# Four neighbouring channels to a chunk row, alpha doubled on ScalarE, two queues for the last rows: one change to a two-branch kernel

## The chip, the core and the metric

The kernel runs on one core of a Trainium2 chip. Its time is the device time of one execution in microseconds (us). An execution under the profiler lists each instruction of the engines: TensorE (PE; its weight loads are PEld), VectorE (DVE), ScalarE (ACT), GpSimd (POOL) and the issuing queue SyncE (SP). A name with a q (SPq, ACTq, POOLq) stands for what the engine's queue does beside computing, issuing DMAs above all. The granted clock is the share of TensorE's full clock that it was given.

## What is computed

Two independent branches over 2048 positions and 640 channels are laid side by side in the output. Branch A is attention with 32 heads of 20 dimensions in a window of 8 keys, two positions apart:

```python
qkv = (x @ wqkv).reshape(B, S, 3, H, Dh)            # H = 32, Dh = 20
idx = pos[:, None] - (jnp.arange(8) * 2)[None, :]
attn = softmax(where(idx >= 0, einsum("bhsd,bhswd->bhsw", q, k[idx]) * scale, -1e9))
a = einsum("bhsw,bhswd->bhsd", attn, v[idx]).reshape(B, S, D) @ wo
```

Branch B is a state space convolution (S4) with 192 complex states a channel:

```python
dt = exp(log_dt)[:, None]
K = einsum("dn,dnl,dn->dl", C, exp(dt * A[:, :, None] * l), dt * B).real   # a filter of 2048 for each channel
y = irfft(rfft(u, 2L) * rfft(K, 2L))[:L] + u * Dskip
```

## The kernel before, in words

**Branch B** works in five chunks of 128 channels (NCH = 5, c = 0 to 4; LAST = 4). The 640 channels are split as g (4 groups of 160), u (4), t (8) and c (5, innermost): chunk c holds every fifth channel. On the partitions stand 32 rows (g, t) for each u. `load` (L122) brings each of the six parameter arrays with four DMAs, one for each u, on the queues of SP, ACT and GpSimd; a partition's five channels are neighbours in memory, one run of 5 x 192 elements. `decays` (L162) turns dt times A_re to columns on TensorE and writes alpha (float32, 4 x 48 numbers a partition and chunk). `fill` (L169) makes the phases on VectorE and moves them with DMAs, `weights` and `coefficients` make C times B.

For each chunk `exps_chunk` (L236) fills the table R on ScalarE with exponentials of multiples of alpha. From chunk 1 on it writes 2 alpha into the place of the previous chunk's alpha (L248, a GpSimd addition), and one ACTIVATE (L251) then reads both. `phase_table` (L267) makes sines in the tables TA and TX (TensorE L288 and L292, ScalarE L296). `small_half` (L310) multiplies tables on VectorE (PG, Q, X; all L317), `y_form` (L341) makes Y (L347), and `kgen_unit` (L351) contracts X and Y on TensorE (L360, L365) into 32 values of l1 by 64 of l0 for each of 8 t in 4 g: one of four units u of the filter K, copied by ScalarE into Ksb (L366). `fwd` (L369) is the forward transform, of u (`fwd_u`) or of K (`transform`): four pieces of eight channels in a first stage (TensorE L379, ScalarE L380), four in a second (L386, L387). Piece b reads channels 8b to 8b + 7 in the chunk's order, which for K is unit b. `products` and `inverse_a` (L408, L417) multiply the spectra and do half of the inverse transform into memory (Z). `times_d` (L436) multiplies half a chunk of u by Dskip into UD (one buffer, ten calls; VectorE L441), and GpSimd's queue stores it (L442).

**Branch A** then projects k, q and v on TensorE, makes products on VectorE and logits, softmax, and in `av_step` (L666) the products of attention and v (VectorE L679), summed on TensorE. `Inverse.part` (L757) is a piece of the second half of branch B's inverse transform: TensorE, a ScalarE copy into ysb (through L473), and after each third part four stores. `out_piece` (L707) is the projection by wo of a block of rows, with a copy into ob and a store of each of its row blocks (L728). From the twelfth piece on (`late`) all stores go by SP.

**The order of work.** A planner orders each engine's instructions by cost estimates, except what is wrapped in `keep_in_program_order` or `issue_after`. From `att.in_order()` on TensorE and ScalarE keep program order. There the loop over six groups of eight steps (L984 to L1009) puts in parts of the inverse transform and output pieces by hand: FILLS gives for a step n how many pieces of `rest` (output) and of `parts` (inverse) follow it; in group 0 the parts come ahead of the step's av_step. `sums` (the softmax's denominators for the second half) come at steps 8, 10, 12 and 14.

Of the kernel before, what the change touches and what calls it, by code (L numbers as in the profile page):

```python
# [10 lines left out]
A = mybir.AluOpType  # L11
ACT = mybir.ActivationFunctionType
# [4 lines left out]
NCH = 5  # L17
# [78 lines left out]
def partB_prep(tc, pools, prm):  # L96
# [12 lines left out]
    alpha = flat[:, 3616:5536].bitcast(f32).rearrange("p (c u w) -> p c u w", c=NCH, u=4)  # L109
    V.memset(early[96:128, :].bitcast(f32), 1.0019378662109375)  # L110
    V.memset(flat[96:128, 0:1536].bitcast(f32), 1.0019378662109375)
    ldt = pl.tile([128, NCH], bf16, name="ldt")
    lsrc = prm["B_log_dt"].rearrange("(g u t c) -> u g t c", g=4, u=4, t=8)
    late = tc.keep_in_program_order
    one = pl.tile([128, 2], f32, name="one")
    nc.gpsimd.memset(one[:], 0.0)
    for u in range(4):
        late((nc.scalar, nc.sync)[u % 2].dma_start(out=ldt[32 * u:32 * u + 32, :], in_=lsrc[u]))
    nat = {}
    F1n, F32n = table_consts_np()  # L120

    def load(nm):  # L122
        nat[nm] = (pl if nm == "B_A_re" else pd).tile([128, NCH, 192], bf16, name=nm, tag=nm)
        src = prm[nm].rearrange("(g u t c) n -> u g t (c n)", g=4, u=4, t=8)
        for u in range(4):
            queue = {"B_A_re": (nc.scalar, nc.sync)[u % 2], "B_A_im": nc.gpsimd, "B_B_im": nc.gpsimd, "B_C_im": nc.gpsimd, "B_C_re": (nc.gpsimd, nc.sync)[u // 2]}.get(nm, nc.sync)
            late(queue.dma_start(out=nat[nm][32 * u:32 * u + 32].rearrange("p c n -> p (c n)"), in_=src[u]))

    load("B_A_re")
    load("B_A_im")  # L130
# [8 lines left out]
    dtb = pl.tile([128, NCH], bf16, name="dtb")  # L139
    late(nc.scalar.activation(out=dtb[:], in_=ldt[:], func=ACT.Exp))  # L140
    dtc = pl.tile([128, NCH], f32, name="dtc")
    V.tensor_copy(out=dtc[:], in_=dtb[:])
    dts = pools["fft"].tile([128, NCH], f32, name="dts")
    V.tensor_scalar(out=dts[:], in0=dtc[:], scalar1=4.0 / 3.0, scalar2=None, op0=A.mult)
    id32 = cpool.tile([128, 32], bf16, name="id32", tag="id32")
# [90 lines left out]
def exps_chunk(tc, pools, B, c):  # L236
    nc = tc.nc
    flat = pools["tab"].tile([128, 9216], bf16, name="R", tag=f"R{c % 2}")
    RA = flat[:, 0:3072].rearrange("p (h g q a f) -> p h g q a f", h=2, g=2, a=8, f=4)
    RX = flat[:, 3072:9216].rearrange("p (q e f) -> p q e f", e=32, f=4)  # L240
    al = B["alpha"][:, c]
    by_half = al.rearrange("p (h v) (q f) -> p h (v q) f", h=2, f=4)
    src = al.rearrange("p u (q f) -> p (u q) f", f=4)
    nc.gpsimd.memset(flat[:, 0:3072].rearrange("p (x a f) -> p x a f", a=8, f=4)[:, :, 0, :], 1.0)
    nc.gpsimd.memset(RX[:, :, 31, :], 1.0)
    if c > 0:
        twice = B["alpha"][:, c - 1]
        nc.gpsimd.tensor_tensor(out=twice, in0=al, in1=al, op=A.add)  # L248
        both = B["alpha"][:, c - 1:c + 1]
        both = both.rearrange("p e u (q f) -> p (u q) e f", f=4)  # L250
    exp = lambda o, i, m: nc.scalar.activation(out=o, in_=i, func=ACT.Exp, scale=m)  # L251
# [12 lines left out]
    return RA, RX  # L264
# [171 lines left out]
def times_d(tc, pools, C, UDd, c, i):  # L436

    nc = tc.nc
    U = C["U"][:].rearrange("p l (ut c) -> p c l ut", c=NCH)[:, c]
    UD = pools["tabb"].tile([128, 32, 32], bf16, name="UD", tag="UD")  # L440
    tc.keep_in_program_order(nc.vector.tensor_tensor(out=UD[:], in0=U[:, 32 * i:32 * i + 32], in1=bc(C["Dsb"][:, c], 1, 32), op=A.mult))  # L441
    nc.gpsimd.dma_start(out=UDd[c, :, 1024 * i:1024 * i + 1024], in_=UD[:].rearrange("p l j -> p (l j)"))  # L442


def fwd_u(tc, pools, C, c, place):

    U = C["U"][:].rearrange("p l (ut c) -> p c l ut", c=NCH)[:, c]
    return fwd(tc, pools, C, (lambda ut: U[:, :, ut]), 0, pools["fft"], place)


S = 2048; D = 640; H = 32; DH = 20; W = 8; DIL = 2; HALO = 14
# [3 lines left out]
class Attention:  # L455
# [251 lines left out]
    def out_piece(self, rows, last=False):  # L707
# [17 lines left out]
        if whole:  # L725
            self.copy(out=ob.rearrange("p (h n) -> p h n", h=2), in_=ps)
        for k in range(ns):
            (nc.gpsimd, nc.sync)[late or k % 2].dma_start(out=self.out_a[512 * (s0 + k) + i0:512 * (s0 + k) + i0 + ni, :], in_=ob[ni * k:ni * k + ni])  # L728
# [5 lines left out]
class Inverse:  # L734
# [22 lines left out]
    def part(self, half, lo, n):  # L757
# [12 lines left out]
        self.att.copy(out=ysb[:, lo:lo + n].rearrange("p l (ut c) -> p l ut c", c=NCH), in_=ps[:, 0:160 * n].rearrange("p (l c ut) -> p l ut c", l=n, c=NCH))  # L770
# [8 lines left out]
def body(tc, ctx, pools, prm, B_u, B_Dskip, Sd, Zd, UDd, A_x, A_wqkv, A_wo, out_a, out_b):  # L779
# [14 lines left out]
    with tc.tile_pool(name="prep_l", bufs=1) as pl, tc.tile_pool(name="prep_d", bufs=1) as pd, tc.tile_pool(name="prep_g", bufs=1) as pg, tc.tile_pool(name="prep_h", bufs=1) as ph, tc.tile_pool(name="psum_p", bufs=2, space=bass.MemoryType.PSUM) as psp:  # L794
# [19 lines left out]
        B["coefficients"](0, psp)  # L814
        B["decays"](1, NCH)
        B["weights"](1, NCH)
        nc.gpsimd.tensor_copy(out=Dsb[:], in_=Dn[:].rearrange("p (ut c) -> p c ut", c=NCH))
# [5 lines left out]
    P1 = P2 = None  # L823

    def transform(c):
        Sk[c] = fwd(tc, pools, C, (lambda ut: Kb[c][:, ut, :]), 1, fp, "sa" if c == LAST else "ss")[0]

    def spectrum(c):
        P1 = fwd_u(tc, pools, C, c, "sa")[0]
# [144 lines left out]
    def fill(some, n=1):  # L974
        for f in some[0:n]:
            f()
        del some[0:n]
# [100 lines left out]
```

## Time and profile before

| | |
|---|---|
| runs | 424.67, 425.53 and 406.79 us, median 424.67 |
| profiled execution | 407.56 us |
| its span (first to last instruction) | 405.8 us |
| mean granted clock of TensorE | 0.954 |
| busy share: PE, DVE, ACT, POOL | 86%, 91%, 76%, 25% |
| chain that ended last, by engine | PE 38%, ACT 21%, DVE 18%, issue 15%, DMA 3%, POOL 2% |

A row of a timeline gives start, duration, engine, source line, operation, what it writes and reads, how many instructions the row merges, and in brackets how long the engine was idle before it and what ended that idle time. A row of a group gives the count, the busy time, the mean duration of one in ns, and the idle time before them. A row of the view by stretches gives the stretch, its length, the busy time (and number) for PE, PEld, DVE, ACT and POOL, the granted clock, the share of the DMA engines' time and GB/s.

### The profile page before, as it was taken

How to read it: one execution, taken by the hardware profiler on the slowest of the kernel's cores; microseconds unless marked ns; L12 is line 12 of the kernel's file. 1: busy time of each engine (PE TensorE's matmuls, PEld its weight loads, DVE VectorE, ACT ScalarE, POOL GpSimd, SP SyncE). 2: the span in 40 equal slices, each digit the busy share in tenths (PEclk: the TensorE clock that was granted, in tenths of full speed). 3: DMA queues.
4: the chain of work that ended last, by engine and by line, in shares of the span. 5: the costliest groups of instructions: out<-in, count | busy, mean ns of one | idle time of the engine just before them, and what ended most of it. 6: DMA issues, size and time to landing. Idle time of an engine off the chain costs nothing.

```text
span 405.8 us, 18754 instructions
## 1 busy us (share of the span) xinstructions
PE 349.7 (86%) x8565; PEld 260.6 (64%) x8565; DVE 370.3 (91%) x350; ACT 307.9 (76%) x532; POOL 100.6 (25%) x114
## 2 busy tenths in 40 slices
PE   1279779979898789889988989999999999899994
PEld 0267667878786679768787666656755676335652
DVE  7999999999989999999799999997967899889961
ACT  2996999879999999989999576533778544845662
POOL 8771049000101000399801000100020030302220
PEclk9999989989989999988999999999999999958998
DMA  5599102132044002420039655301652264797542
GB/s 143 155 235 193 22 4 107 57 81 56 29 151 115 3 3 81 135 55 2 31 112 152 124 93 133 100 4 24 214 162 79 104 160 107 209 254 222 163 125 74
DMA packets 40839, 43.36 MB, mean 107 GB/s; under 512 B 24144, under 2 KB 34288, under 8 KB 40120
## 3 DMA queue, kind: packets, MB, share of 16 engines
q1 hardware_dynamic: 35960, 30.60, 31.3%
q0 software_dynamic: 4656, 11.44, 9.3%
q8 instruction: 67, 1.10, 1.1%
q10 hardware_dynamic: 144, 0.12, 0.1%
q14 instruction: 12, 0.10, 0.1%
HBM read 19.69 MB, written 14.16 MB: 83 GB/s over the span
## 4 chain that ended last, share of the span: by engine, by line
PE 38%; ACT 21%; DVE 18%; issue 15%; DMA 3%; POOL 2%; SPq 1%; ACTq 0%; DVEq 0%; POOLq 0%
ACT R L251 8%; DVE X L317 6%; DVE Y L347 5%; PE ps_q L556 5%; PE ps_k L538 4%; PE ps_v L569 4%; DVE PG L317 3%; PE ps_x L472 3%; PE ps_o L472 3%; PE ps_op L472 3%; ACT A L380 3%; PE ps_ph L288 3%; PE ps_k L360 2%; POOL LPB L248 2%; DVE Q L317 2%
## 5 line engine op out<-in xcount | busy, mean ns | idle before, releaser
L347 DVE TENSOR_TENSOR Y<-PG 128x3072 bf16<-128x3072 bf16 x60 | 103.0, 1754 | 4.1 <-PE ps_k L365 4.1
L251 ACT ACTIVATE R<-LPB 128x192 bf16<-128x192 f32 (+1 forms) x185 | 56.5, 409 | 0.6 <-POOL LPB L248 0.5
L360 PE MATMUL ps_k<-Y,X 128*32 128x64 bf16 x1920 | 46.3, 239 | 10.3 <-DVE Y L347 9.5
L248 POOL TENSOR_TENSOR LPB<-LPB 128x192 f32<-128x192 f32 x4 | 45.9, 11470 | 29.4 <-ACT R L251 25.8
L288 PE MATMUL ps_ph<-LPB,LPA 128*64 128x256 bf16 x320 | 35.1, 323 | 12.7 <-DMA LPA<-lo 7.8
L360 PEld LDWEIGHTS <-X 128*32 128x32 bf16 x1920 | 32.8, 117 | 19.7 <-issue 8.9
L387 ACT CAST A<-ps_f 128x1024 bf16<-128x1024 f32 x40 | 37.6, 1036 | 7.4 <-PE ps_f L386 7.4
L365 PE MATMUL ps_k<-Y,X 64*32 64x64 bf16 x1920 | 42.9, 233 | 0.0
L380 ACT CAST A<-ps_f 128x1024 bf16<-128x1024 f32 x40 | 37.7, 1041 | 0.6 <-PE ps_f L379 0.6
L317 DVE TENSOR_TENSOR X<-R,TX 128x1536 bf16<-128x1536 bf16 x40 | 37.7, 963 | 0.3 <-DMA LPA<-hi 0.3
L386 PE MATMUL ps_f<-A,T 128*64 128x128 bf16 x640 | 29.1, 258 | 8.5 <-ACT A L380 8.4
L365 PEld LDWEIGHTS <-X 64*32 64x32 bf16 x1920 | 29.5, 112 | 8.6 <-issue 0.9
L386 PEld LDWEIGHTS <-T 128*64 128x64 bf16 x640 | 27.1, 129 | 10.1 <-issue 9.1
L679 DVE TENSOR_TENSOR prod<-v,atp 128x1536 bf16<-128x1536 bf16 (+3 forms) x32 | 30.9, 1023 | 2.4 <-PE ps_o L472 1.2
L296 ACT ACTIVATE TX<-ps_ph 128x768 bf16<-128x768 int16 x40 | 30.0, 836 | 1.1 <-PE ps_ph L292 1.0
L296 ACT ACTIVATE TA<-ps_ph 128x768 bf16<-128x768 int16 x40 | 29.7, 815 | 0.5 <-PE ps_ph L292 0.2
L288 PEld LDWEIGHTS <-LPA 128*64 128x64 bf16 x320 | 18.3, 124 | 17.0 <-DMA LPA<-hi 7.9
L589 DVE TENSOR_TENSOR prod<-qT,kT 128x1024 bf16<-128x1024 bf16 (+1 forms) x16 | 22.9, 1482 | 4.2 <-ACT qT L557 4.2
L292 PE MATMUL ps_ph<-LPB,LPA 128*64 128x128 bf16 x320 | 24.1, 246 | 0.0
L442 POOL DMA_DIRECT2D UDdram<-UD x10 | 5.5, 551 | 72.4 <-DVE UD L441 65.7
L538 PE MATMUL ps_k<-xT,wkq 128*128 128x512 bf16 x100 | 22.9, 379 | 0.2 <-ACT A L387 0.2
L556 PE MATMUL ps_q<-xT,wkq 128*128 128x512 bf16 x100 | 22.6, 379 | 0.0
(157 smaller groups left out, 733.3 us busy)
## 6 DMA issues: line engine op xcount, KB each, us to landing
P<-A SPq DMA_DIRECT2D x16, 256.0 KB
Zdram<-Z SPq DMA_DIRECT2D x16, 256.0 KB
Z<-Zdram SPq DMA_DIRECT2D x30, 128.0 KB
U<-in_B_u_dram SPq DMA_DIRECT2D x4, 640.0 KB
UDdram<-UD POOLq DMA_DIRECT2D x10, 256.0 KB, 2.3
out_dram<-ysb SPq DMA_DIRECT2D x32, 80.0 KB
Z<-UDdram SPq DMA_DIRECT2D x16, 128.0 KB
Z<-Zdram POOLq DMA_DIRECT2D x10, 128.0 KB, 4.8
```

Of the source, the lines that this page charges most:

```text
L248: nc.gpsimd.tensor_tensor(out=twice, in0=al, in1=al, op=A.add)
L251: exp = lambda o, i, m: nc.scalar.activation(out=o, in_=i, func=ACT.Exp, scale=m)
L288: MM(o[64 * hh:64 * hh + 64, :, 0:8], lhsT=L[:, 64 * hh:64 * hh + 64], rhs=rhs, start=first, stop=last, skip_group_check=True, tile_positi ...
L296: last = nc.scalar.activation(out=dst, in_=words.rearrange("p b (q e f) -> p b q (e f)", e=8, f=4), func=ACT.Sin, scale=PI_LO / 32768.0)
L317: TT = lambda o, a, b, op: V.tensor_tensor(out=o, in0=a, in1=b, op=op)
L347: nc.vector.tensor_tensor(out=Y[:].rearrange("p q (b a) f -> p q b a f", a=8), in0=fa, in1=gb, op=A.mult)
L360: MM(ps[32 * g:32 * g + 32, t], lhsT=X[:, q, k, :, f], rhs=Ys[k][:, q, :, f], start=(t == 0 and k == 0), stop=False, tile_position=(0, 32 ...
L365: MM(ps[32 * g:32 * g + 32, t], lhsT=X[hb, q, k, :, f], rhs=Ys[k][hb, q, :, f], start=False, stop=(k == 2), tile_position=(64 * (g // 2), ...
L380: nc.scalar.copy(out=A1[:, 8 * b:8 * b + 8], in_=ps[:])
L386: last = MM(ps[sl, kk], lhsT=C["T2"][:, 8 * b + kk, sl], rhs=A1[:, :, 8 * b + kk, :], start=(kk % 4 == 0), stop=True, skip_group_check=Tru ...
L538: MM(ps[:, i], lhsT=self.wk[:, kt, 128 * ct:128 * ct + 128], rhs=self.x4[:, kt, 2 * i:2 * i + 2, 256 * hf:256 * hf + 256], start=(kt == 0) ...
L556: MM(ps[:, i], lhsT=self.wq[:, kt, 128 * ct:128 * ct + 128], rhs=self.x4[:, kt, 2 * i:2 * i + 2, 256 * hf:256 * hf + 256], start=(kt == 0) ...
```

## The change

1. The 640 channels are split as g (4), t (8), c (5), u (4): chunk c of a row of twenty channels holds four neighbours. Each parameter load then has rows of 192 elements instead of 960, log dt comes whole (20 columns on every partition), its exponential is written in place, and dtc is picked by four copies. The views of u, K, Dskip and ysb follow. In K's transform, channel n of a chunk lies in unit n mod 4.
2. 2 alpha is written by a ScalarE ACTIVATE (Copy, scale 2).
3. The late stores are shared: the first half of a piece's row blocks by SP, the second by ScalarE's queue, all output stores in program order.
4. FILLS has other numbers (the same 24 parts and the same pieces), at step 7 and step 16 among them; at step 7 the parts come behind the av_step; `sums` come at steps 9, 11, 13 and 14.

```diff
-    ldt = pl.tile([128, NCH], bf16, name="ldt")
-    lsrc = prm["B_log_dt"].rearrange("(g u t c) -> u g t c", g=4, u=4, t=8)
+    ldt = pl.tile([128, 4 * NCH], bf16, name="ldt")
+    lsrc = prm["B_log_dt"].rearrange("(p x) -> p x", x=4 * NCH)
...
-        src = prm[nm].rearrange("(g u t c) n -> u g t (c n)", g=4, u=4, t=8)
+        src = prm[nm].rearrange("(p c u) n -> u p c n", c=NCH, u=4)
...
-    late(nc.scalar.activation(out=dtb[:], in_=ldt[:], func=ACT.Exp))
+    late(nc.scalar.activation(out=ldt[:], in_=ldt[:], func=ACT.Exp))
+    dtb = ldt[:].rearrange("p (c u) -> p c u", u=4)
...
-    V.tensor_copy(out=dtc[:], in_=dtb[:])
+    for u in range(4):
+        V.tensor_copy(out=dtc[32 * u:32 * u + 32, :], in_=dtb[32 * u:32 * u + 32, :, u])
...
-        nc.gpsimd.tensor_tensor(out=twice, in0=al, in1=al, op=A.add)
+        nc.scalar.activation(out=twice, in_=al, func=ACT.Copy, scale=2.0)
...
-    U = C["U"][:].rearrange("p l (ut c) -> p c l ut", c=NCH)[:, c]
+    U = C["U"][:].rearrange("p l (t c u) -> p c l t u", c=NCH, u=4)[:, c]
...
-    tc.keep_in_program_order(nc.vector.tensor_tensor(out=UD[:], in0=U[:, 32 * i:32 * i + 32], in1=bc(C["Dsb"][:, c], 1, 32), op=A.mult))
+    by_t = lambda ap: ap.rearrange("p l (t u) -> p l t u", u=4)
+    tc.keep_in_program_order(nc.vector.tensor_tensor(out=by_t(UD[:]), in0=U[:, 32 * i:32 * i + 32], in1=by_t(bc(C["Dsb"][:, c], 1, 32)), op=A.mult))
...
-            (nc.gpsimd, nc.sync)[late or k % 2].dma_start(out=self.out_a[512 * (s0 + k) + i0:512 * (s0 + k) + i0 + ni, :], in_=ob[ni * k:ni * k + ni])
+            queue = (nc.sync, nc.scalar)[k * 2 // ns] if late else (nc.gpsimd, nc.sync)[k % 2]
+            self.tc.keep_in_program_order(queue.dma_start(out=self.out_a[512 * (s0 + k) + i0:512 * (s0 + k) + i0 + ni, :], in_=ob[ni * k:ni * k + ni]))
...
-        Sk[c] = fwd(tc, pools, C, (lambda ut: Kb[c][:, ut, :]), 1, fp, "sa" if c == LAST else "ss")[0]
+        Sk[c] = fwd(tc, pools, C, (lambda n: Kb[c][:, 8 * (n % 4) + n // 4, :]), 1, fp, "sa" if c == LAST else "ss")[0]
...
-    FILLS = {1: (0, 2), 3: (0, 2), 5: (0, 1), 7: (0, 1), 9: (0, 1), 11: (0, 2), 13: (0, 2), 15: (0, 1), 17: (1, 0), 19: (2, 2), 23: (1, 2), 27: (2, 2), 31: (2, 2), 35: (2, 2), 37: (0, 2), 39: (1, 0), 43: (1, 0), 45: (1, 0)}
+    FILLS = {1: (0, 1), 3: (0, 1), 5: (0, 2), 7: (0, 2), 11: (0, 2), 13: (0, 1), 15: (0, 2), 16: (0, 1), 17: (1, 0), 19: (2, 2), 23: (1, 2), 27: (2, 2), 31: (2, 2), 35: (2, 2), 37: (0, 2), 39: (1, 0), 43: (1, 0), 45: (1, 0)}
...
-                fill(parts, FILLS.get(n, (0, 0))[1])
+                if w < 7:
+                    fill(parts, FILLS.get(n, (0, 0))[1])
...
-            if n in (8, 10, 12, 14):
-                k = (8, 10, 12, 14).index(n)
+            if n in (9, 11, 13, 14):
+                k = (9, 11, 13, 14).index(n)
...
-            if group > 0 and n in FILLS:
+            if n > 6 and n in FILLS:
```

More of the change, by code (lines that the diff above doesn't have):

```diff
@@ L117, in partB_prep @@
     for u in range(4):
-        late((nc.scalar, nc.sync)[u % 2].dma_start(out=ldt[32 * u:32 * u + 32, :], in_=lsrc[u]))
+        late((nc.scalar, nc.sync)[u % 2].dma_start(out=ldt[32 * u:32 * u + 32, :], in_=lsrc))
     nat = {}
@@ L123, in load @@
         nat[nm] = (pl if nm == "B_A_re" else pd).tile([128, NCH, 192], bf16, name=nm, tag=nm)
-        src = prm[nm].rearrange("(g u t c) n -> u g t (c n)", g=4, u=4, t=8)
+        src = prm[nm].rearrange("(p c u) n -> u p c n", c=NCH, u=4)
         for u in range(4):
             queue = {"B_A_re": (nc.scalar, nc.sync)[u % 2], "B_A_im": nc.gpsimd, "B_B_im": nc.gpsimd, "B_C_im": nc.gpsimd, "B_C_re": (nc.gpsimd, nc.sync)[u // 2]}.get(nm, nc.sync)
-            late(queue.dma_start(out=nat[nm][32 * u:32 * u + 32].rearrange("p c n -> p (c n)"), in_=src[u]))
+            late(queue.dma_start(out=nat[nm][32 * u:32 * u + 32], in_=src[u]))
     load("B_A_re")
@@ L438, in times_d @@
     nc = tc.nc
-    U = C["U"][:].rearrange("p l (ut c) -> p c l ut", c=NCH)[:, c]
+    U = C["U"][:].rearrange("p l (t c u) -> p c l t u", c=NCH, u=4)[:, c]
     UD = pools["tabb"].tile([128, 32, 32], bf16, name="UD", tag="UD")
-    tc.keep_in_program_order(nc.vector.tensor_tensor(out=UD[:], in0=U[:, 32 * i:32 * i + 32], in1=bc(C["Dsb"][:, c], 1, 32), op=A.mult))
+    by_t = lambda ap: ap.rearrange("p l (t u) -> p l t u", u=4)
+    tc.keep_in_program_order(nc.vector.tensor_tensor(out=by_t(UD[:]), in0=U[:, 32 * i:32 * i + 32], in1=by_t(bc(C["Dsb"][:, c], 1, 32)), op=A.mult))
     nc.gpsimd.dma_start(out=UDd[c, :, 1024 * i:1024 * i + 1024], in_=UD[:].rearrange("p l j -> p (l j)"))
 def fwd_u(tc, pools, C, c, place):
-    U = C["U"][:].rearrange("p l (ut c) -> p c l ut", c=NCH)[:, c]
-    return fwd(tc, pools, C, (lambda ut: U[:, :, ut]), 0, pools["fft"], place)
+    U = C["U"][:].rearrange("p l (t c u) -> p c l t u", c=NCH, u=4)[:, c]
+    return fwd(tc, pools, C, (lambda n: U[:, :, n // 4, n % 4]), 0, pools["fft"], place)
 S = 2048; D = 640; H = 32; DH = 20; W = 8; DIL = 2; HALO = 14
@@ L769, in part @@
                 self.att.MM(ps[32 * s:32 * s + 32, 160 * i:160 * (i + g1 - g0)].rearrange("p (g c n) -> p g c n", c=NCH, n=32), lhsT=self.HB[:, 16 * qr + l, :], rhs=self.t[qr][:, g0:g1, :, l, :], start=(i == 0), stop=True, skip_group_check=True, tile_position=(0, 32 * s))
-        self.att.copy(out=ysb[:, lo:lo + n].rearrange("p l (ut c) -> p l ut c", c=NCH), in_=ps[:, 0:160 * n].rearrange("p (l c ut) -> p l ut c", l=n, c=NCH))
+        self.att.copy(out=ysb[:, lo:lo + n].rearrange("p l (t c u) -> p l c t u", c=NCH, u=4), in_=ps[:, 0:160 * n].rearrange("p (l c t u) -> p l c t u", l=n, c=NCH, u=4))
         if lo + n == 8:
@@ L816, in body @@
         B["weights"](1, NCH)
-        nc.gpsimd.tensor_copy(out=Dsb[:], in_=Dn[:].rearrange("p (ut c) -> p c ut", c=NCH))
+        nc.gpsimd.tensor_copy(out=Dsb[:].rearrange("p c (t u) -> p c t u", u=4), in_=Dn[:].rearrange("p (t c u) -> p c t u", c=NCH, u=4))
     psg = ctx.enter_context(tc.tile_pool(name="psum_g", bufs=2, space=bass.MemoryType.PSUM))
```

1 line of the change is left out of this document (removed).

## The prediction

> **What bounds the kernel now.** I read the page first (busy shares, the chain that ended last), then the chain in order of time, then busy time by stretch, then each engine's timeline around the lines that the change touches. The stretches from 64 to 229 us, where four of the five chunks are worked off:
>
> ```profile
> PE 349.7 (86%) x8565; PEld 260.6 (64%) x8565; DVE 370.3 (91%) x350; ACT 307.9 (76%) x532; POOL 100.6 (25%) x114
> ...
> 64.20:88.30 24.10, 21.66 (x718) 18.52 (x713) 22.53 (x20) 19.48 (x25) 7.39 (x5) 1.00 0.28 91
> 88.30:128.40 40.10, 36.95 (x1075) 32.34 (x1070) 38.17 (x29) 39.86 (x74) 3.73 (x7) 0.92 0.30 84
> 128.40:178.90 50.50, 44.52 (x1375) 37.45 (x1377) 50.50 (x42) 47.92 (x85) 10.27 (x5) 0.97 0.23 64
> 178.90:200.90 22.00, 18.92 (x584) 16.25 (x586) 21.57 (x17) 20.46 (x36) 22.00 (x2) 0.92 0.02 4
> 200.90:229.20 28.30, 25.43 (x732) 21.86 (x721) 25.76 (x21) 26.55 (x47) 2.92 (x5) 0.94 0.67 134
> ```
>
> After the stretch's length stand the busy times of PE, PEld, DVE, ACT and POOL. By the page alone DVE (91%) is the bound and ACT (76%) has room. By stretch that is not so: from 88 to 179 us ACT is busy 87.8 of 90.6 us and DVE 88.7. The two are in lockstep, and work taken from one moves the end only as far as the other follows. That decides what the change is worth.
>
> **VectorE's product u times D (L441).** Ten instructions, each with a channel step of five elements today and runs of four neighbours after the change.
>
> ```profile
> L441 DVE TENSOR_TENSOR UD<-U,Dsb 128x1024 bf16<-128x1024 bf16 x10 | 13.5, 1348 | 3.5 <-DMA UDdram<-UD 3.5
> L317 DVE TENSOR_TENSOR PG<-Q 128x1536 bf16<-128x1536 bf16 x10 | 9.5, 955 | 0.0
> L317 DVE TENSOR_TENSOR PG<-PG 128x768 bf16<-128x768 bf16 x20 | 11.4, 572 | 0.0
> L347 DVE TENSOR_TENSOR Y<-PG 128x3072 bf16<-128x3072 bf16 x60 | 103.0, 1754 | 4.1 <-PE ps_k L365 4.1
> ```
>
> The two L317 rows give (955 - 572) / 768 = 0.50 ns an element and 0.19 us fixed, so 1024 elements at that rate take 0.70 us; L441 takes 1.35. L347 reads runs of four neighbours, as L441 would, and lies on the fast line (0.19 + 3072 x 0.50 = 1.72). I take 0.70: ten times 0.65 saved, 6.5 us of DVE. The bounds are 0 (it stays at 1.35) and 6.5.
>
> **Alpha doubled by ScalarE instead of GpSimd (L248).**
>
> ```profile
> 56.05 13.88 POOL L248 TENSOR_TENSOR LPB<-LPB 128x192 f32<-128x192 f32 x1 [18.98 <-ACT R L251]
> 170.32 30.51 POOL L248 TENSOR_TENSOR LPB<-LPB 128x192 f32<-128x192 f32 x1
> 200.78 0.56 POOL L442 DMA_DIRECT2D UDdram<-UD  x1
> 203.31 1.30 DVE L441 TENSOR_TENSOR UD<-U,Dsb 128x1024 bf16<-128x1024 bf16 x1 [2.84 <-DMA UDdram<-UD]
> 200.87 2.52 ACT L251 ACTIVATE R<-LPB 128x384 bf16<-128x384 f32 x7 [0.54 <-POOL LPB L248]
> 43.43 3.66 ACT L251 ACTIVATE R<-LPB 128x192 bf16<-128x192 f32 x14
> L222 ACT ACTIVATE CN<-p,dts 128x192 bf16<-128x192 f32 x4 | 1.7, 464 | 0.0
> ```
>
> L248 lasted until VectorE paused, up to 30.5 us. Behind it on GpSimd's queue stands the store of UD (L442), and VectorE's next L441 waits for that store, since UD has one buffer: 2.84 us here, 3.5 in all. Both waits go, and ACT's 0.54 too. In their place ScalarE runs four copies of 192 elements. The nearest row is L251's (3.66 / 14 = 0.26 us each), the upper end L222's 0.46: +1.05 us of ACT, at most 1.9. [...]
>
> **The transform of K waits for all four units.** transform(c) today reads unit b for its piece b; with the new order of channels piece 0 already reads all four units.
>
> ```profile
> 81.56 1.53 PE L379 MATMUL ps_f<-BD,Ksb 128*64 128x128 bf16 x48
> 81.69 0.58 ACT L366 CAST Ksb<-ps_k 128x512 bf16<-128x512 f32 x1 [0.37 <-PE ps_k L365]
> 82.24 3.76 ACT L380 CAST A<-ps_f 128x1024 bf16<-128x1024 f32 x4
> 88.26 3.76 ACT L387 CAST A<-ps_f 128x1024 bf16<-128x1024 f32 x4 [2.26 <-PE ps_f L386]
> 178.91 0.58 ACT L366 CAST Ksb<-ps_k 128x512 bf16<-128x512 f32 x1 [1.40 <-PE ps_k L365]
> ```
>
> Three pieces (48 matmuls) run while ScalarE still copies the last unit, and L380 follows that copy at once. After the change the first piece starts at 82.27 and takes 1.53 / 3 = 0.51 us, so L380 would come about 0.75 us later with its semaphores. That occurs for chunks 0, 1 and 2; chunk 3's transform comes long after its units. TensorE can put other matmuls in, ScalarE may find other work: 0 to 0.75 each, I take 0.4, so +1.2.
>
> **What the stage gives.** DVE has 6.5 + 3.5 = 10 us less to do. But chunk 4's first products need tables from ScalarE:
>
> ```profile
> 225.12 1.76 DVE L317 TENSOR_TENSOR PG<-R,TA 128x3072 bf16<-128x3072 bf16 x1
> 222.85 0.81 ACT L296 ACTIVATE TA<-ps_ph 128x768 bf16<-128x768 int16 x1 [0.24 <-PE ps_ph L292]
> 223.58 3.09 ACT L296 ACTIVATE TX<-ps_ph 128x768 bf16<-128x768 int16 x4
> ```
>
> TA ends at 223.66, so PG at 225.12 can come 1.46 us earlier plus whatever ACT gains. ACT: +1.05 (alpha) + 1.2 (transforms) - 0.54 (no L248) - 0.8 of the 2.26 wait at 88 (TensorE's L386 there stands behind a Y of VectorE; the rest is the time from L380 to L386) - 0.5 of the 1.40 at 178.9 = +0.4. The stage gains 1.46 - 0.4 = 1.0 us; the other 9 us of VectorE turn into waits for TA and TX. Bounds: -8 (rival one) and +3 (all ACT costs at their upper ends, no wait shorter: 1.9 + 2.25 - 0.54 = 3.6, with 0.6 of cover left).
>
> **Parameter loads in rows of 384 bytes.** Each of the 24 loads has 160 rows of 384 bytes instead of 32 rows of 1920.
>
> ```profile
> 3.60 5.80 DMA B_A_re<-in_B_A_re_dram
> 10.08 11.50 ACT R L251 x45
> ...
> DMA  0122646999753445439699997499999999999999
> GB/s 0 25 32 62 147 143 196 268 333 225 138 141 123 142 132 149 105 94 257 197 393 316 316 226 209 120 265 196 187 191 174 186 188 216 216 184 217 192 174 182
> ```
>
> The last B_A_re load lands at 9.40 and the 45 exponentials hang on it: a delay there goes one for one to the end. The lower rows are slices of 1 us. From 30 to 40 us U's rows of 320 bytes move at about 190 GB/s with the engines full; the loads reach 333. So 60 KB take 0.32 instead of 0.18 us, and the eight loads ahead of the landing (A_re, A_im) 1.1 us more where the engines are full; they are half full for most of it, so +0.7. Bounds: 0, and 5.8 x (333 / 190 - 1) = +4.4 if all of the 5.80 stretches. [...]
>
> **Costed at nothing.** Four copies of dtc instead of one (+0.35 us on DVE) end before the last B_A_re has landed; if that cover went, they would cost 0.35. The exponential on 20 instead of 5 columns, the reordered Dsb and ysb copies and the reordered weights of L379 handle the same or hardly more elements with the same engine.
>
> **TensorE's fillers.** Two parts of the output transform move from before proj_v(18) to after it, two more from before the last sums to after them.
>
> ```profile
> 350.13 3.56 DVE L679 TENSOR_TENSOR prod<-v,atp 128x1536 bf16<-128x1536 bf16 x4 [1.16 <-ACT v L473]
> 360.25 1.76 DVE L637 RECIPROCAL soft<-ps_x 128x256 bf16<-128x256 f32 x1 [1.34 <-PE ps_x L472]
> 352.56 0.36 PE L472 MATMUL ps_o<-prod,ident 32*32 32x384 bf16 x8 [0.97 <-ACT o L473]
> 353.48 0.38 PE L472 MATMUL ps_x<-lsb,ident 128*128 128x256 bf16 x2 [0.56 <-ACT o L473]
> 358.21 0.99 PE L472 MATMUL ps_ib<-Z,HB 96*32 96x480 bf16 x12
> ```
>
> VectorE's two waits (2.5 us) should go: two parts fewer are about 2 us of TensorE ahead of each. TensorE's own work is the same, so it gains only what it stands idle: 0.97 + 0.56 at the border of groups 0 and 1, into which the two parts after step 7 fall. I take TensorE's 1.5; bounds -2.5 and +0.5 (a part put at step 16 delays group 2).
>
> **The last rows.** SP issues 16 row blocks one after the other; now SP and ACT issue eight each.
>
> ```profile
> 399.77 0.49 DVE L705 CAST ob<-ps_o 128x320 bf16<-128x320 f32 x1 [0.87 <-PE ps_o L472]
> 401.88 1.17 SPq L728 DMA_DIRECT2D out_dram<-ob  x2
> 2.70 1.30 ACTq L127 DMA_DIRECT2D B_A_re<-in_B_A_re_dram  x2
> ```
>
> The last data are there at 400.26, the last issue ends at 403.05: up to 2.1 us of queue. On ACT an issue takes 0.65 (third row) and stands in front of ScalarE's copies: seven issues between 394 and 400 us, of which its idle time takes about half, so the last copy comes about 0.6 later. Gain 1.5; bounds 2.1, and a loss of 1.0 if ScalarE's issues come fully on top.
>
> **Sum.** +0.7 - 1.0 - 1.5 - 1.5 = -3.3 against the profiled execution's 407.56 us (span 405.8): 404.3 us. Of the runs shown one lies at 406.79 and two at 424.67 and 425.53, 4% above the profiled execution, and no row here says why; at the median's level the same forecast is 404.3 x 424.67 / 407.56 = 421.3.
>
> **Rivals.** (1) ScalarE follows VectorE. ACT is idle 10.7 us of the 165 from 64 to 229; if those waits were mostly for matmuls that wait for VectorE, 8 of the 10 us come through: 404.3 - 7.0 = 397.3. For it: the 2.26 wait. Against it: 88 to 128 us, where ACT is busy 39.86 of 40.10. Chance 0.2. (2) Slower: the small rows decide. If B_A_re's landing takes twice as long, +5.8 instead of +0.7: 409.4; from 4.0 us on it eats all other gains. For it: the landing heads the chain and nothing hides it. Against: the engines are half idle at 3 to 7 us. Chance 0.15. (3) Fillers and tail give nothing, because TensorE stays full and ScalarE's issues delay its copies as much as SP's queue did: 407.3. Chance 0.2.
>
> **How the numbers follow.** The forecast has 0.45 and its own range 400 to 408. With the rivals 397 to 410 holds 8 in 10 at the profiled level; since two of three runs shown lie 4% higher, the range goes up to the forecast at that level, 422. Two per cent (8 us) is about what a measurement of this kernel tells from no change. Faster by more: rival one and the low edge of the forecast, 0.22. Slower by more: rival two far beyond its price, or an order of work that I do not see, 0.12. Within: 0.66.
>
> **What would show it.** L441 at 0.70 us; L248 gone from POOL, no wait of L441 on its store; VectorE waiting for TA or TX at chunk 4 (if not, rival one); a wait of ACT L380 on L379; the landing of B_A_re and the start of the exponentials (10.08 now); no wait at L637; the last issue right behind the last copy. I am wrong if ACT's waits shrink with VectorE's work, or if the loads land some microseconds later.

## The result and the profile after

The changed kernel takes 402.95 us in the median of six runs (401.90 to 405.34); the kernel before takes 424.81 beside it (406.79 to 425.53). The ratio of comparable runs is 0.9896 (95% interval 0.9871 to 0.9921). Two more measurements gave 0.9910 (0.9869 to 0.9950) and 0.9906 (0.9871 to 0.9942), so about 1% or 4 us. To understand the medians: 55 of the 158 runs of the kernel before in this study took 423 to 434 us instead of 404 to 413, no run of the changed kernel did, and the ratio compares the others.

The profiled execution after took 401.9 us (span 400.1, before 405.8). These starts in us are read from the two timelines:

| | before | after |
|---|---|---|
| first exponential (ScalarE) | 10.08 | 8.37 |
| first product of chunk 0 (VectorE) | 28.34 | 28.24 |
| first product of chunk 4 | 225.12 | 222.88 |
| first product of the logits | 271.90 | 269.67 |
| first product of the last av group | 386.51 | 381.52 |
| last copy into ob | 399.77 | 395.97 |

The table's steps in rows of the timelines after (line numbers there are one to four higher than before), first ScalarE's tables, then VectorE at chunk 4 and at the logits:

```profile
8.37 2.89 ACT L252 ACTIVATE R<-LPB 128x192 bf16<-128x192 f32 x11
26.20 1.51 ACT L297 ACTIVATE TA<-ps_ph 128x768 bf16<-128x768 int16 x2 [3.51 <-PE ps_ph L293]
219.88 2.92 ACT L297 ACTIVATE TA<-ps_ph 128x768 bf16<-128x768 int16 x4
222.66 2.95 ACT L297 ACTIVATE TX<-ps_ph 128x768 bf16<-128x768 int16 x4
```

```profile
222.88 1.76 DVE L318 TENSOR_TENSOR PG<-R,TA 128x3072 bf16<-128x3072 bf16 x1 [2.44 <-ACT TA L297]
269.67 3.69 DVE L588 TENSOR_TENSOR prod<-ql,kT 128x1024 bf16<-128x1024 bf16 x6
```

The exponentials start 1.71 us earlier, but ScalarE waits 3.51 us for the phases at 26 us, and chunk 0's product comes where it was. At chunk 4 VectorE has run out of work and waits 2.44 us for TA, as forecast.

The groups by tile and line, after: UD and alpha, with the durations as least, median and greatest in ns.

```profile
L443 DVE TENSOR_TENSOR UD<-U,Dsb x10: 685/687/708, 64.8 to 199.4; 128x1024 bf16<-128x1024 bf16 x10
L249 ACT ACTIVATE LPB<-LPB x4: 393/407/442, 41.5 to 193.4; 128x192 f32<-128x192 f32 x4
```

UD takes 0.69 us (forecast 0.70). Alpha takes 0.41 us on ScalarE, where the forecast had 0.26. That was the spacing of fourteen exponentials of the same size that overlap (3.66 / 14); each of them lasts 0.35 (the median of L251 before).

The end after: SyncE's queue, ScalarE's and the last copy.

```profile
388.25 8.79 SPq L731 DMA_DIRECT2D out_dram<-ob  x10
```

```profile
395.97 0.49 DVE L707 CAST ob<-ps_o 128x320 bf16<-128x320 f32 x1 [0.87 <-PE ps_o L474]
396.53 0.53 ACTq L731 DMA_DIRECT2D out_dram<-ob  x1
```

The last issue ends 0.60 us after the last copy; before, it ended 2.78 us after.

### The profile page after: what moved, and what is told of

It is laid out like the page before. It is cut to its first block, busy times and chain, and to the rows that moved or that the text cites. A ratio compares the mean times of both kernels' runs of the same rounds, so it can differ in the third digit from the quotient of the medians.

```text
span 400.1 us, 18758 instructions
## 1 busy us (share of the span) xinstructions
PE 345.0 (86%) x8565; PEld 258.7 (65%) x8565; DVE 363.8 (91%) x353; ACT 308.4 (77%) x536; POOL 53.5 (13%) x110
## 4 chain that ended last, share of the span: by engine, by line
PE 46%; ACT 37%; DVE 10%; issue 3%; DMA 2%; SPq 1%; ACTq 0%; DVEq 0%
ACT R L252 10%; ACT A L381 8%; ACT A L388 6%; PE ps_ph L289 5%; PE ps_q L558 5%; PE ps_k L540 4%; PE ps_k L366 4%; PE ps_k L361 4%; PE ps_v L571 4%; PE ps_f L387 3%; PE ps_x L474 3%; ACT Z L429 3%; PE ps_o L474 2%; PE ps_ia L428 2%; PE ps_l L602 2%
## 5 line engine op out<-in xcount | busy, mean ns | idle before, releaser
L289 PE MATMUL ps_ph<-LPB,LPA 128*64 128x256 bf16 x320 | 33.6, 313 | 8.8 <-DMA LPA<-lo 6.6
L293 PE MATMUL ps_ph<-LPB,LPA 128*64 128x128 bf16 x320 | 23.0, 241 | 0.0
L318 DVE TENSOR_TENSOR PG<-R,TA 128x3072 bf16<-128x3072 bf16 x10 | 17.5, 1754 | 5.0 <-ACT TA L297 5.0
L380 PE MATMUL ps_f<-BD,U 128*64 128x128 bf16 x320 | 20.5, 286 | 0.8 <-ACT Z L429 0.6
```

The source lines that it names most:

```text
L289: MM(o[64 * hh:64 * hh + 64, :, 0:8], lhsT=L[:, 64 * hh:64 * hh + 64], rhs=rhs, start=first, stop=last, skip_group_check=True, tile_positi ...
L318: TT = lambda o, a, b, op: V.tensor_tensor(out=o, in0=a, in1=b, op=op)
```

## The experiments

### Each part alone

Four kernels, each the kernel before with one part of the change. Theory "lockstep": VectorE and ScalarE hold each other up to 229 us, so that a part which relieves one alone gives less than it does together with the others. Theory "sum of work": each part gives its own term.

```diff
# e_alpha
-        nc.gpsimd.tensor_tensor(out=twice, in0=al, in1=al, op=A.add)
+        nc.scalar.activation(out=twice, in_=al, func=ACT.Copy, scale=2.0)
# e_chan: all of the change's part 1
-        src = prm[nm].rearrange("(g u t c) n -> u g t (c n)", g=4, u=4, t=8)
+        src = prm[nm].rearrange("(p c u) n -> u p c n", c=NCH, u=4)
...
# e_fill: FILLS, step 7 and the places of sums
-            if n in (8, 10, 12, 14):
+            if n in (9, 11, 13, 14):
...
# e_tail
-            (nc.gpsimd, nc.sync)[late or k % 2].dma_start(
+            queue = (nc.sync, nc.scalar)[k * 2 // ns] if late else (nc.gpsimd, nc.sync)[k % 2]
...
```

> The kernel before with one part of the change: 2 alpha is written by ScalarE, not by GpSimd. Theory lockstep (VectorE and ScalarE limit each other from 64 to 229 us, so that work taken from one moves the end only as far as the other follows): VectorE's two waits for the store of UD (3.5 us) go, ScalarE has 4 x 0.41 us more, the end comes 1 to 2 us earlier, 405.5 to 406.5 us. Theory sum of work (VectorE alone sets the end): 3.5 us earlier, 404 us. On the two levels at which the kernel before was timed (407 and 425 us): if the upper one comes from GpSimd's addition, which lasts until VectorE pauses, no run of this kernel is above 410; if it has another cause, about half of them are near 425.

> The kernel before with the new split of channels alone (runs of four neighbours, log dt whole and in place, GpSimd still doubles alpha). Lockstep: VectorE's product with D takes 0.69 instead of 1.35 us ten times, but chunk 4's first product waits for ScalarE's table TA; K's transform waits for its last unit (0.56 us, four times); -1 to +1 us, 406.5 to 408.5. Sum of work: -6.5 us, 401 us. The exponentials of chunk 0 start near 8.4 us instead of 10.1 because log dt is there earlier; that shows in the profile whatever the time is. If GpSimd's addition makes the upper level of the runs, it is still there in this kernel.

> The kernel before with the new places of TensorE's fillers alone. After minus before, the profiles differ by 2.8 us between 345 and 376 us of the span; if that is the fillers' own, this kernel gains 2 to 3 us, 404.5 to 405.5. The prediction's bound was TensorE's idle time at the border of the groups, 1.5 us. Rival: it only follows from the stages before, then 0.

> The kernel before with the last rows on two queues alone. Predicted 1.5 us gain from the queue's 2.1. From the profiles after and before the last stage gives 0.7 us only, because ScalarE's issues stand before its copies: 406.5 to 407. Rival: issues on ScalarE cost as much as the queue on SP, 0.

Measured: 0.9989 (0.9953 to 1.0024), 1.0014 (0.9982 to 1.0047), 0.9984 (0.9949 to 1.0018), 1.0012 (0.9987 to 1.0037). No part gives anything that shows by itself, and "sum of work" falls: it had 3.5 us for alpha and 6.5 for the channels. (For the fillers the interval still holds the forecast 1.5 us, 0.9963.) But the profiles of e_alpha and e_chan are 3.9 and 5.1 us ahead of before at 200 us and lose it at 219 to 226 us, where TensorE stands still in the middle of K's matmuls. Part of that lead would have ended in a wait for TA in any case (after is 4.6 us ahead at 200 us and 2.2 at chunk 4), but not all. The rows of e_alpha, then e_chan, then after, on both sides of the same place in the program:

```profile
224.13 0.36 PE L360 MATMUL ps_k<-Y,X 128*32 128x64 bf16 x12 [2.42 <-issue]
```

```profile
218.89 0.23 PE L361 MATMUL ps_k<-Y,X 128*32 128x64 bf16 x3
222.13 0.36 PE L361 MATMUL ps_k<-Y,X 128*32 128x64 bf16 x12 [3.01 <-issue]
```

```profile
219.73 0.67 PE L361 MATMUL ps_k<-Y,X 128*32 128x64 bf16 x29 [0.37 <-issue]
```

Behind this wait ScalarE gets the phases for the last piece of TA late (e_alpha, then e_chan; after has no such wait):

```profile
225.16 0.81 ACT L296 ACTIVATE TA<-ps_ph 128x768 bf16<-128x768 int16 x1 [3.00 <-PE ps_ph L292]
```

```profile
223.31 0.81 ACT L297 ACTIVATE TA<-ps_ph 128x768 bf16<-128x768 int16 x1 [1.52 <-PE ps_ph L293]
```

"issue" means that no semaphore explains the wait. Counted in the trace, TensorE's instruction 10177 waits in all three. The page of the profile after has for the queues

```profile
q8 instruction: 67, 1.10, 1.1%
```

that is 67 packets of 16 KB (1.10 MB / 67) for TensorE's 17,130 matmuls and weight loads, by my estimate a block of 256 instructions each (17,130 / 67 = 255.7). 10177 is 39 x 256 + 193, and other such waits of these traces fall on 5313, 6593, 7617 and 8129, all with the remainder 193 (in the profile after 1.12 us at 5313, 1.41 at 6593, 0.78 at 7617). I read that as TensorE having come to the end of what it holds. The view of the DMA queues for e_chan (packets, MB, share of the 16 engines' time; a packet counts whole where it starts, so a share can pass 100%), from 216 to 219 us and then from 219.5 to 220.7 us:

```profile
q0 software_dynamic: 120, 0.48, 77.3%
q1 hardware_dynamic: 394, 0.14, 18.3%
```

```profile
q1 hardware_dynamic: 480, 0.16, 187.1%
q8 instruction: 1, 0.02, 5.2%
```

GpSimd's 480 KB load of the k weights (q0) takes 77.3% of the engines' time from 216 to 219 us; the block's packet starts only behind it, at 219.59. In e_alpha the load ends at 220.88 and the packet starts at 221.76; in after it starts at 217.39, together with the load (217.38), and the wait is short (0.37 us, against 2.42 in e_alpha and 3.01 in e_chan).

### Parts in pairs, and the weight load moved

```diff
# e_chan_w (on e_chan) and e_alpha_w (on e_alpha): load_x
-        behind(self.tc, nc.gpsimd.dma_start(out=self.wk[:, :, 256:D], ...), ins)
...
                last = ins
+                if (hf, q) == (0, 3):
+                    behind(self.tc, nc.gpsimd.dma_start(out=self.wk[:, :, 256:D], ...), ins)
```

e_ac is e_alpha and e_chan together, e_ft is e_fill and e_tail together, a_again is the changed kernel.

> The changed kernel once more, on the chip of the next three runs, so that they are compared with it and with the kernel before under the same conditions. Every theory: 402 to 404 us, 0.987 to 0.992 of before's lower level. What it tells apart is the wait inside the matmuls of K (TensorE's instruction 10177, right after VectorE's Y is ready): 0.37 us in the first profile. Theory "supply" (TensorE runs out of instructions there when their block of 16 KB stands behind the 480 KB load of the k weights): it depends on where that load falls, so 0 to 1 us again. Theory "chance" (one execution was unlucky): anything up to 3 us.

> The kernel before with alpha on ScalarE and the channel split (with log dt in place), without the fillers and the two queues of the last rows. Theory "stage" (the two together take 2.2 us out of the stage up to 229 us, which neither does alone, and the rest comes behind it): logits start at about 269.7 us instead of 271.9, time 405.0 to 405.6, ratio 0.994 to 0.996. Theory "all four" (nothing of it arrives without the fillers): 407, ratio 0.998 to 1.002. If TensorE's wait for instructions at 10177 is 2 to 3 us here as in each part alone, the first theory's gain is gone as well, and the profile shows that wait in its place.

> The kernel before with the new filler places and the two queues, without the other two parts: the work up to the first logits is that of before. If these two parts give their 2.8 + 0.7 us by themselves: first logits at 271.9, 403.5 to 404.5 us, ratio 0.990 to 0.993. Each alone gave nothing (0.9984 and 1.0012): if that holds together, 406.5 to 407.5, ratio 0.998 to 1.001, and the 3.5 us between the first logits and the end of the changed kernel come from something that the earlier stage leaves behind (a later granted clock, other places of loads).

> The channel split alone, with one edit more: the 480 KB load of the k weights is put behind the fourth of the transposed loads of x (it then moves at about 227 us instead of 216 to 219 us, and is read first at about 235). Theory "supply": in the run without this edit TensorE stood still for 3.01 us from 219.12 us, its block of instructions started moving at 219.59, when the load was through, and VectorE's first product of chunk 4 came at 224.21. Without the load in front of it the block comes two microseconds earlier, the wait falls below 1 us, the product comes at 221.5 to 222.5, and the time falls by 1.5 to 2.4 us, ratio 0.994 to 0.997 instead of 1.0014. Theory "chance": the wait has nothing to do with that load, the ratio stays at 1.000 to 1.002 and the wait is there or not as it happens.

> Alpha on ScalarE alone, with the 480 KB load of the k weights behind the fourth transposed load of x, the edit that took the channel split alone from 1.0014 to 0.9955. Theory "supply": here too TensorE's wait inside K's matmuls (2.42 us at 221.7 us) goes, and the ratio falls from 0.9989 to 0.993 to 0.996. Rival: the gain in the other case came from something else that the load's new place brings (the k projection's own start); then it may be the same size here, but the wait at TensorE's instruction 10177 would be as long as it was.

Measured: e_ac 0.9950 (0.9924 to 0.9977), e_ft 0.9969 (0.9930 to 1.0008). Alpha and channels together give what the first logits show (269.95 us), and it arrives at the end; the two pairs multiply to 0.992, near a_again's 0.991. e_chan_w: 0.9955 (0.9922 to 0.9988); e_alpha_w: 0.9987 (0.9949 to 1.0025). At the same instruction they show

```profile
221.10 0.36 PE L361 MATMUL ps_k<-Y,X 128*32 128x64 bf16 x12 [0.61 <-issue]
```

```profile
218.99 0.36 PE L360 MATMUL ps_k<-Y,X 128*32 128x64 bf16 x12 [0.54 <-issue]
```

so by these four waits (0.61 after 3.01 us, 0.54 after 2.42) the load was what held the block back. The price isn't settled: the intervals of e_chan and e_chan_w meet, and the two were timed on different chips. In e_alpha_w the first product of chunk 4 came at 221.89 instead of 226.06, yet the time is that of e_alpha. In e_chan_w the ratio is lower, yet the product came at 224.19, missing the forecast 221.5 to 222.5: ScalarE was 1.6 us later there for waits further ahead.

### What the fillers give back

In the profiles with the new fillers TensorE waits for the third of the four quarters in which the output transform's input Z is loaded. The rows are of after and of a_third; the releaser named is the last DMA event of a wait for eight semaphores of SyncE's queue.

```profile
365.54 0.59 PE L474 MATMUL ps_ib<-Z,HB 96*32 96x480 bf16 x12 [1.44 <-DMA out_dram<-ysb]
```

```profile
367.08 0.59 PE L474 MATMUL ps_ib<-Z,HB 96*32 96x480 bf16 x12 [3.18 <-DMA out_dram<-ysb]
```

```diff
# a_z: the third quarter's loads on two queues
-                (nc.sync, nc.gpsimd)[(c + ri) % 2 if qr in (0, 3) else 0].dma_start(
+                (nc.sync, nc.gpsimd)[(c + ri) % 2 if qr != 1 else 0].dma_start(
# a_zg: a_z, and
-            queue = (nc.sync, nc.scalar)[k * 2 // ns] if late
+            queue = (nc.sync, nc.gpsimd)[k * 2 // ns] if late
# a_y: the first four stores of ysb by GpSimd (a_yw: and the moved weight load)
-                nc.sync.dma_start(out=self.dst[...
+                (nc.gpsimd if half == 0 else nc.sync).dma_start(out=self.dst[...
```

> The changed kernel with one edit more: the 15 loads of Z for the third quarter of the output transform are issued by SyncE and GpSimd in turn, as those of the first and the last quarter are, instead of by SyncE alone. Theory "given back": with the fillers in their new places TensorE comes to the third quarter some 5 us earlier than before, and there stands still until SyncE has issued its loads, behind the four stores of ysb (1.44 and 2.94 us in the two profiles of the changed kernel, 0.99 and 3.37 in the two with the fillers alone, none in the kernels with the old places). With half of the loads on another queue that wait goes, and the time falls by 1 to 2.5 us: ratio to the kernel before 0.984 to 0.989 instead of 0.990. Rival "full anyway": TensorE's wait only replaces one for VectorE's products a little later, and the ratio stays at 0.989 to 0.992.

> As a_z, and half of the last row blocks are issued by SyncE and half by GpSimd, not by ScalarE. In the six profiles with ScalarE's issues or without them, the time from the last group's first product to the end is 18.3 to 19.4 us with two queues and 19.2 to 19.7 us (once 20.8) with one: the queue's 2.1 us are won, but the last copy comes 0.9 to 2.0 us later, since seven issues of 0.6 us stand in front of ScalarE's copies. Theory "ScalarE pays": with GpSimd's issues (0.53 us each, beside nothing) the last copy comes when it came before, and the end 0.8 to 1.5 us earlier than in a_z: ratio 0.981 to 0.987. Rival "GpSimd's queue lands later": its transfers take some microseconds from issue to landing, and what the copies win is lost at the end: same as a_z or up to 2 us worse.

> The changed kernel a third time, on the chip of the next three runs, as what they are compared with. 0.986 to 0.993 of the kernel before; its third profile shows once more how far two executions of the same kernel lie apart (span 400.1 and 404.9 us so far): TensorE's wait at the third quarter of the output transform should be there again, 1 to 3 us.

> The changed kernel with one edit: the first four stores of ysb are issued by GpSimd instead of SyncE, so that SyncE's loads of Z for the third quarter are not queued behind them. Theory "given back": SyncE has issued the last of these loads at about 359 us instead of 363 to 366, TensorE's wait for them (1.44 and 2.94 us) goes, without the loads of two quarters moving at once, which gave a new wait of 2.99 us at 351 us in the other attempt; time 1 to 2 us below the changed kernel on the same chip (ratio to before 0.984 to 0.988 where that has 0.990). Rival "full anyway": VectorE or ScalarE's copies take the place, the wait is gone and the time is the same within 0.3%.

> As the one before, and the 480 KB load of the k weights behind the fourth transposed load of x. In the two profiles of the changed kernel TensorE's wait inside K's matmuls at 219 us is 0.37 and below 0.9 us, so by theory "supply" the edit can give at most that: 0 to 0.8 us on top. If it gives 1.5 us or more, that load costs something else as well; it took 0.6% off the channel split alone and nothing off alpha on ScalarE alone, in whose profile the wait was gone nevertheless.

Measured: a_z 0.9862 (0.9809 to 0.9914, six runs), a_third 0.9906, a_y 0.9870 (0.9807 to 0.9933, six runs), a_yw 0.9898 (0.9863 to 0.9933). None is told apart from the changed kernel. The profiles say why; a_z, then a_y:

```profile
354.31 0.85 PE L474 MATMUL ps_ib<-Z,HB 96*32 96x480 bf16 x12 [2.99 <-DMA Z<-UDdram]
```

```profile
366.93 0.59 PE L474 MATMUL ps_ib<-Z,HB 96*32 96x480 bf16 x12 [2.50 <-DMA out_dram<-ysb]
```

In a_z the wait moved to an earlier part; in a_y it stayed, although no store stood in front of SyncE's loads: the quarter's last load went out at 361.26 us (361.95 in the profile after). My theory that the stores in the queue hold them falls: the quarter lands at 365 to 369 us by either order, and the fillers only bring TensorE there earlier. What holds the loads stays open.

a_zg: 1.0046 (1.0013 to 1.0078), the rival's outcome and worse. The last copy starts at 395.33, its last issue is

```profile
396.39 0.53 POOL L731 DMA_DIRECT2D out_dram<-ob  x1 [0.81 <-issue]
```

but the span is 405.9: 9.0 us from the end of that issue, against 3.0 after ScalarE's last. The store isn't what fills them: it landed at 398.57. The rows of GpSimd's DRAIN at the end of the program (L1077) fill them; a_zg, then after:

```profile
L1077 POOLq DRAIN  x3: 46/102/8797, 396.4 to 405.7; - x3
```

```profile
L1077 POOLq DRAIN  x3: 46/102/7583, 387.2 to 399.9; - x3
```

The longest of the three begins with GpSimd's last issue. It takes 7.58 to 8.80 us in all twenty profiles; elsewhere GpSimd's last store is issued early enough that the DRAIN is over before the other queues are (at 399.82 us before, where SyncE's last issue ends at 403.05, and at 394.83 after, where ScalarE's ends at 397.06). So the rival's outcome holds, but not its reason, a late landing.

### One of the two late parts left out

```diff
# a_nt, a_nt2: the changed kernel, last stores by SyncE alone
-            queue = (nc.sync, nc.scalar)[k * 2 // ns] if late else (nc.gpsimd, nc.sync)[k % 2]
+            (nc.gpsimd, nc.sync)[late or k % 2].dma_start(
...
# a_nf: the changed kernel, FILLS and sums as before
-                if w < 7:
...
```

> The changed kernel with the last row blocks issued by SyncE alone, as before the change: alpha, the channel split and the fillers stay. By the prediction's 1.5 us for the two queues: 1.5 us slower than the changed kernel, 0.37%. By the profiles' time from the last group's first product to the end (18.3 to 19.4 us with two queues, 19.2 to 19.7 with one): 0.5 us, within the scatter. If it is as fast or faster, the two queues are worth nothing and all that the changed kernel gains comes from the other parts.

> The changed kernel with the fillers in their old places: alpha, the channel split and the two queues of the last rows stay. By the prediction's 1.5 us for the fillers: 0.9945 of the kernel before (the changed kernel had 0.9896 to 0.991). By the rows: TensorE reaches the third quarter of the output transform at 363 to 364 us with the new places and waits there until that quarter's loads land at 365.5 to 369, whichever queue issues them; with the old places it reaches it at 368 to 370 and does not wait. By that the fillers are worth what they bring the groups ahead, 0 to 1 us: 0.990 to 0.993. The queues alone: the kernel without them had 0.9964, so if fillers and queues add up, 0.995 (alpha and channels) minus 0.006 = 0.989 means that the fillers are worth nothing.

> The changed kernel without the two queues once more, on the same chip as the kernel without the new filler places, so that each of the two is known beside the same runs of the kernel before. 0.9964 before; if the two queues are worth 0.5% again, 0.994 to 0.998, and above the other kernel of this call. If it comes out below it, the difference between 0.9964 and 0.9906 was scatter, and the fillers carry the gain.

Measured: a_nt 0.9964 (0.9924 to 1.0003), a_nt2 0.9963 (0.9925 to 1.0001), a_nf 0.9953 (0.9919 to 0.9987). Either part alone on top of alpha and channels (0.9950) gives nothing that shows; the step to 0.9906 is seen with both together, and it is small beside the intervals, which overlap (the means without each kernel's longest run, all on one chip, are 406.1 us for e_ac, 404.6 for a_again and 404.8 for a_third). Their single shares stay open: each interval is some 0.7% wide, and two profiles of the changed kernel differ by 4.8 us of span.

### The runs at 425 us

```diff
# e_dsb
-        nc.gpsimd.tensor_copy(out=Dsb[:], in_=Dn[:]...
+        nc.scalar.copy(out=Dsb[:], in_=Dn[:]...
```

> The kernel before with one edit: the copy of Dsb runs on ScalarE instead of GpSimd. Of the 69 runs of the kernel before in the two earlier calls 25 took 423.7 to 433.9 us and the rest 405.4 to 410; of the 48 runs of kernels with alpha on ScalarE or the channel split none did. The profile of one such run (fillers and two queues alone, 427.86 us) has a single difference of that size: the copy of Dsb on GpSimd takes 32.17 us (0.37 us otherwise) beside VectorE's unbroken work, the addition of alpha stands behind it on GpSimd, and ScalarE waits 19.05 us for that. Theory "GpSimd starved": without the copy on GpSimd no run of this kernel lies at 424 us, and the others are where they were, or 0.3 us later for the copy on ScalarE: ratio 0.999 to 1.002. Rival: the level belongs to the chip or to another place, and 4 of 12 runs are at 424 us again.

Measured: seven of twelve runs at 427 to 430 us, the others at 1.0005 (0.9963 to 1.0046). The copy of Dsb can't be the only cause; the rival's half about the place holds. GpSimd and ScalarE in e_dsb's profile:

```profile
36.41 31.00 POOL L248 TENSOR_TENSOR LPB<-LPB 128x192 f32<-128x192 f32 x1 [5.46 <-ACT LPB L167]
```

```profile
67.44 4.51 ACT L251 ACTIVATE R<-LPB 128x384 bf16<-128x384 f32 x13 [19.51 <-POOL LPB L248]
```

The addition of alpha itself takes 31.00 us instead of 0.50, beside VectorE's unbroken products, and ScalarE waits 19.51 us for it. In e_ft it was the copy ahead of it (32.17 us), with the same wait (19.05). Both ended within 0.4 us of the end of VectorE's unbroken stretch, at 67.05 and 64.60 us; so did the ten other GpSimd instructions of over 13 us in the profiles with the addition on GpSimd (those of 13.88 and 30.51 us in the profile before 0.38 and 0.36 us after it). What lets such an instruction through early in the other executions is not shown: in the profile before the addition ran in a pause of VectorE (0.30 us, at 36.5 us), but in e_fill and e_tail it took 1.09 and 1.22 us with no such pause, and the product of VectorE beside it took 1.26 instead of 0.95 (in the kernel before, the third of the four additions passed in 1.00 us at 125.83 us, again with no pause, and a product there took 2.05 instead of 1.76). In this study 14 of 48 runs of the other kernels with the addition on GpSimd and the old channel split (e_fill, e_tail, e_ft, e_dsb) lie there, beside 55 of 158 of the kernel before; of 134 with alpha on ScalarE none does (24 of them have no other part of the change), nor of 24 with the channel split and alpha on GpSimd. So either of the two parts keeps the level away; how the channel split does it stays open (in its two profiles the first addition took 0.67 and 0.92 us).

## Why the prediction was right or wrong

**The sum.** Forecast -3.3 us against the profiled 407.56, that is 0.992; measured 0.9896 to 0.9910, whose intervals hold it, and 402.95 us for 404.3. The size came out by luck: errors of both signs met (loads and stage together -2.0 instead of -0.3, fillers and queues -1.8 instead of -3.0). Wrong was the sentence that the same forecast at the median's level would be 421.3, and with it the upper end of the range: a median of 424.8 became 402.95.

**The step that failed there** was "no row here says why". This row of the profile before, the view of line L248, pointed at it:

```profile
L248 POOL TENSOR_TENSOR LPB<-LPB x4: 499/7436/30512, 36.6 to 170.3; 128x192 f32<-128x192 f32 x4
```

The same addition takes 0.50 to 30.5 us, and the first of the four stands on ScalarE's path. I costed its removal at the 0.54 us that ScalarE waited in this one execution; in about a third of the others the wait that goes is 19 us, by the profiles of e_ft and e_dsb. A rival "alpha off GpSimd removes the long executions" was missing.

**Loads, +0.7.** Wrong in sign, and without effect: the exponentials start 1.71 us earlier, since log dt is issued in 0.44 instead of 0.96 us on ScalarE's queue, the four B_A_re loads follow sooner, and the last of them lands at 6.58 instead of 9.40, 3.66 instead of 5.80 us after its issue; chunk 0's first product moves by 0.10, because ScalarE waits 3.51 us for the phases. So the step "a delay there goes one for one to the end" fails, and the bound "0" left out a gain without a reason.

**Stage, -1.0.** Mis-sized: -2.0 with the loads, by e_ac's 0.9950 and by the first logits at 269.0 to 270.6 us in the ten profiles with both parts and the old weight load, against 271.90. The cover of 1.46 was right (the bound +3 took off only 0.6 of it; by its own numbers it is 3.6 - 1.46 = +2.1). The failed step is "ACT = +0.4": TA's end moved from 223.66 to 222.80, 0.9 the other way, although alpha cost 1.6 instead of 1.05, because ScalarE's waits shrank by more than I took: from 30 us to that end of TA it stood idle 10.3 instead of 13.6 us. So rival one's mechanism was there, at a tenth of its price; the waits of VectorE for TA show that ScalarE stayed the bound.

**Fillers and queues, -1.5 each.** Together 0.9950 to 0.9906, -1.8 instead of -3.0, as far as the intervals tell. Of VectorE's two waits the fillers took one away in the profile after and halved the other (1.16 to 0.54):

```profile
347.28 3.69 DVE L681 TENSOR_TENSOR prod<-v,atp 128x1536 bf16<-128x1536 bf16 x4 [0.54 <-ACT v L475]
356.09 1.75 DVE L639 RECIPROCAL soft<-ps_x 128x256 bf16<-128x256 f32 x1
```

But "TensorE gains what it stands idle" left out what is late next: the third quarter's loads, 1.4 to 3.2 us. From the first logits to the last group's first product it takes 111.6 to 115.1 us in eleven profiles with the new fillers and 112.2 to 115.3 in nine with the old: a gain, if any, is no larger than the scatter. The queues bring the last issue right behind the last copy, as forecast; but from the last group's first product to the end of the last copy it takes 14.6 to 16.9 us with them and 13.8 without (a_nt, e_ac): the 0.6 put on ScalarE's issues was 0.8 to 3.2 against the queue's 2.2. That is the term that was mis-sized.

**Not in the sum:** the waits that I read as TensorE's supply of instructions. Both halves of the stage's change ran into one alone (2.42 and 3.01 us), and the lead in their profiles was gone behind it. That it is all that hid their worth isn't shown: e_alpha_w, without that wait, took the time of e_alpha.

## What to carry to other kernels

Where two levels of time stand in the runs, look in the one profile for an instruction of one shape whose durations differ by a factor of tens (0.50 and 30.51 us here): that is a place to test, and an edit that removes it can be worth the difference of the levels times how often it strikes. Parts measured alone needn't add up; measure them on top of each other before calling one useless. An "issue" wait at a fixed instruction count was here, by my reading, a block of instructions under way (up to 3.01 us): look at what the DMA queues move just then. Where GpSimd issues the last stores, look whether its closing DRAIN stands at the end of the kernel, as in a_zg (8.80 us), and try another queue for them.

## What the runs showed of the hardware

- A GpSimd addition of 128 x 192 numbers took 0.50 us in a pause of VectorE and up to 31.00 us beside VectorE's products; each long one ended within 0.4 us of the end of VectorE's unbroken stretch. In e_fill and e_tail, where the addition passed in 1.09 and 1.22 us, a product of VectorE took 0.31 us longer; in the profile before, where it passed in 1.00 us at 125.83 us, 0.29 us.
- TensorE waited 2.42 and 3.01 us at its instruction 10177 where a 16 KB packet of instructions moved only behind a load of 480 KB on another queue, and 0.54 and 0.61 us with that load moved.
- GpSimd's DRAIN at the program's end took 7.6 to 8.8 us from its last issue. With last stores by GpSimd that made 9.0 us from the last issue to the end, against 3.0 by ScalarE's.
